# Half of pair 4's read issued before pair 3's turn, pair 6 scaled between the masks of pairs 4 and 5, pair 3's output evacuated in four parts

## The chip, the cores and the metric

The kernel runs on one core of one Trainium2 chip. The core has five engines that run side by side, each through its own list of instructions in order: TensorE (PE in the profile; PEld is its weight load), VectorE (DVE), ScalarE (ACT), GpSimd (POOL) and SyncE (SP), which here only issues transfers. The metric is the device time of one execution in microseconds, lower is better; the figure for a kernel is the median over its runs.

## The reference

A chunked state-space scan over 4 sequences of 768 tokens and 8 heads (head dimension 32, state 16) makes a matrix of 3072 tokens by 256. A gated feed-forward network follows. Cut to what matters:

```python
for c in range(nc):                                  # chunks of the sequence
    cum = np.cumsum(log_a[:, :, sl], axis=-1)
    L = np.exp(cum[:, :, :, None] - cum[:, :, None, :]) * causal
    CB = np.einsum('bhin,bhjn->bhij', Cc, Bc)
    y_intra = np.einsum('bhij,bhjd->bhid', CB * L, xc)
    y_inter = np.einsum('bhin,bhnd->bhid', Cc, state) * np.exp(cum)[:, :, :, None]
    y[:, :, sl] = y_intra + y_inter
    state = decay_full * state + np.sum(Bx, axis=2)
x = y.transpose(0, 2, 1, 3).reshape(B * S, H * D)    # 3072 x 256
gate = np.maximum(x @ w_gate, 0.0)                   # 256 x 1536
val = x @ w_val
out = gate * val @ w_out                             # 1536 x 256
```

## The kernel before

Tokens go in 12 pairs of 256 (a pair is two blocks of 128; three pairs make a sequence) for the scan, and in 6 blocks of 512 (two pairs) for the network. Pairs 0 to 3 are read with two neighbouring tokens in a row ("wide"), pairs 4 to 11 one block at a time.

A pair passes these steps. `load` (L107) issues its reads on SP: for pairs from 4 on, B, C and x of block 0, then B, C and x of block 1, six transfers (L120, L121). `scale_bc` (L324; for pair 3 `scale_wide`, L298) multiplies B and C by decay factors on POOL, four multiplies (L333) into one of four token tiles `tok`. `turn_dma` (L290) has SP issue one transposing transfer from `tok` to `turned`. `cast_x` (L340) casts x on POOL. On PE, `G` (`G_wide` for pair 3) forms the products of C and B out of `turned` into four banks of PSUM; `gevac` (L552) brings them to SBUF with the causal mask, two of them by a copy on ACT and a mask on POOL (`causal`, L547), two on DVE; pair 3 uses `gcopy` and `gmask`. `sums` (L573) adds up the states on PE out of `tok` and the cast x; `states` masks them on DVE. `inter` (L617, `inter_full` for pair 3) and `Dm` (L629, `D_wide`) add the parts of y on PE; `yevac` (`yevac_wide` for pair 3, L524) writes y as bf16 to `yT`, a tile of 128 x 2 x 3072 (its second dimension is called t here).

A block of 512 tokens passes `gv` or its half `gvh` (L655, L669) for each f of 12: gate and value products out of `yT` on PE, a relu on ACT, a product on DVE into `h`; then `fout` (L691, 12 matmuls for each of four slices of 128 tokens) and `foevac` (L710), whose writes SP issues. `gvh` takes 256 tokens, so block 1's first half reads pair 2 alone, its second half pair 3.

The order on every engine is the order in which the code is written out: `in_order` (L15) chains all instructions of an engine. So a waiting instruction holds everything behind it on its engine, and SP's list of transfers is one queue. The order around the change is in L869 to L981: after pair 3's scaling come its turn, the six reads of pair 4 and the six of pair 5 (L869 to L871), then two output writes of block 0. In block b = 1 (loop at L914, P = 4, Q = 5) pair 4 is scaled and turned, pair 6 read, pair 5 scaled and turned, pair 7 read (L942 to L949); then `G(4)` and its masks (L959, L962), later `G(5)` and its masks (L975, L976), the last slice's write, and pair 6's scaling, turn and cast (L981). Block 2 reads pairs 8 and 9 first (L917 to L919), then scales pair 7 (L946).

PSUM has a shared pool of five banks for `G`, gate, value and `fout`; `raw` holds four pairs' reads, `att` four `turned` tiles and three casts of x.

Of the kernel before, what the change touches and what calls it, by code (L numbers as in the profile page):

```python
# [8 lines left out]
FP32 = mybir.dt.float32  # L9
# [20 lines left out]
def kernel(  # L30
# [13 lines left out]
    nc = tc.nc  # L44

    NB, NH, S, D = x.shape
    N = B.shape[-1]
# [11 lines left out]
    raw = ctx.enter_context(tc.tile_pool(name="raw", bufs=4))  # L59
# [17 lines left out]
    st = {}  # L77
# [16 lines left out]
    def load_x(p, *qs):  # L94
        xr = raw.tile([128, NH, 2, D], FP32, tag="xr", name="xr")
        if p == 2:
            nc.vector.memset(xr[0:1, 0, 0, 0:1], 0.0)
        b, s0 = p // PPB, p % PPB * 256
        n = NH // len(qs)
        for i, q in enumerate(qs):  # L100
            hs = slice(i * n, (i + 1) * n)
            q.dma_start(out=xr[:, hs].rearrange("p h r d -> p h (r d)"),
                        in_=x[b, hs, s0:s0 + 256, :].rearrange(
                            "h (p r) d -> p h (r d)", r=2))
        st.setdefault(p, {})["xr"] = xr

    def load(p):  # L107
        q = nc.sync
        if p < NWIDE:
            load_bc(p, 1, q)  # L110
            load_bc(p, 0, q)
            load_x(p, q)
            return
        b, c0 = p // PPB, 2 * (p % PPB)
        xr = raw.tile([128, 2, NH, D], FP32, tag="xr", name="xr")
        bcr = raw.tile([128, 2, 2, NH, N], FP32, tag="bcr", name="bcr")
        for i in range(2):
            sl = slice((c0 + i) * 128, (c0 + i + 1) * 128)
            for src, j in ((B, 0), (C, 1)):
                q.dma_start(out=bcr[:, i, j], in_=src[b, :, sl, :].rearrange("h s n -> s h n"))  # L120
            q.dma_start(out=xr[:, i], in_=x[b, :, sl, :].rearrange("h s d -> s h d"))  # L121
        st[p] = {"xr": xr, "bcr": bcr}

    H = S // 2
    HC = NC // 2
# [24 lines left out]
    for rows, base in ((slice(0, 128), 128), (slice(0, 64), 0)):  # L150
        nc.gpsimd.affine_select(
            out=wmask[rows], in_=wmask[rows], pattern=[[-1, 2], [1, 128]],
# [6 lines left out]
    for k in range(4):  # L159
# [16 lines left out]
        out=cp0, data0=a0, data1=zero1[0:R].to_broadcast([R, 128]), initial=1.0,  # L176
# [102 lines left out]
    def scale(p, eng, ceng):  # L279
        scale_bc(p, eng)  # L280
        cast_x(p, ceng)
# [8 lines left out]
    def turn_dma(p):  # L290
        s = st[p]
        bs = tok[p % NTOK]
        s["turned"] = turned = att.tile([128, 6, 128], BF16, tag="turned", name="turned", bufs=4)
        nc.sync.dma_start_transpose(out=turned, in_=bs.rearrange("s k c -> s (k c)"))
        s["BT"] = turned[:, 0:2]
        s["CT"] = turned[:, 2:6].rearrange("s (t i) m -> s t i m", t=2)

    def scale_wide(p, j, eng):  # L298
        s = st[p]
        if p >= FIRST:  # L300
            s["bs"] = bs = tok[p % NTOK]
            src = s["bcr"].rearrange("s (t q) j r n -> s j r t q n", t=2)[:, j]
            for t in range(2):
                k = 2 * j * (1 + t)
                eng.tensor_tensor(
                    out=bs[:, k:k + 2].rearrange("s k (q t n) -> s k t q n", q=4, t=2)[:, :, t],
                    in0=src[:, :, t],
                    in1=fac3[:, j, :, 4 * t:4 * t + 4].to_broadcast([128, 2, 4, N]),
                    op=ALU.mult)
            return  # L310
        if "bs" not in s:
            s["bs"] = bs = att.tile([128, 4, 128], BF16, tag="bs", name="bs")
            s["tin"] = [[bs[:, 2 * j + r] for r in range(2)] for j in range(2)]
        src = s["bcr"].rearrange("s (t q) j r n -> s j r t q n", t=2)[:, j]
        f = wfac[:, j, :, :, p]
        for t in range(2):
            eng.tensor_tensor(  # L317
                out=s["bs"][:, 2 * j:2 * j + 2].rearrange(
                    "s k (q t n) -> s k t q n", q=4, t=2)[:, :, t],
                in0=src[:, :, t],  # L320
                in1=f[:, :, 4 * t:4 * t + 4].to_broadcast([128, 2, 4, N]),
                op=ALU.mult)
# [201 lines left out]
    def yevac_wide(p, *engs):  # L524
        s = st[p]
        for i, eng in enumerate(engs):
            dst = yT[:, :, p * 256 + i * 128:p * 256 + (i + 1) * 128]
            src = s["yw"][i][:, 0:256].rearrange("s (t m) -> s t m", t=2)
            if p >= FIRST:
                dst = dst.rearrange("s t (m r) -> s t r m", r=2)  # L530
                src = src.rearrange("s t (r m) -> s t r m", r=2)
            (eng.copy if eng is nc.scalar else eng.tensor_copy)(out=dst, in_=src)  # L532

    def G(p):
# [66 lines left out]
    def states(p):  # L601
        c = 2 * (p % PPB)
        for k in range(2 if c < NC - 2 else 1):
            S[2 * p + 1 + k] = n = att.tile([128, 2, 128], BF16, tag="Sm", name="Sm", bufs=5)
            shape = [128, 2, 4, D]
            nc.vector.tensor_tensor(  # L606
                out=n.rearrange("s t (q d) -> s t q d", q=4),
                in0=acc["A"][:, k].rearrange("s (t d) -> s t d", t=2).unsqueeze(2)
                .to_broadcast(shape),
                in1=smask.rearrange("s t (q d) -> s t q d", q=4), op=ALU.mult)  # L610
# [80 lines left out]
    def fout(b, ts, fs=range(NF)):  # L691
        if fs[0] == 0 and (ts % 2 == 0 or b == NBLK - 1):
            fst["o"] = bank("o", (128, 2, DM))
        o = fst["o"]
        if b == NBLK - 1 and ts == 3:
            fst["oh"] = [o[:, 1, 0:128], bank("o", (128, 128))]
            for i, oh in enumerate(fst["oh"]):
                for f in range(NF):
                    nc.tensor.matmul(
                        out=oh, lhsT=fst[b][:, f, ts * 128:(ts + 1) * 128],  # L700
                        rhs=wo[:, f, i * 128:(i + 1) * 128], start=(f == 0),
                        stop=(f == NF - 1), skip_group_check=True)
            return
        for f in fs:
            nc.tensor.matmul(  # L705
                out=o[:, ts % 2], lhsT=fst[b][:, f, ts * 128:(ts + 1) * 128],
                rhs=wo[:, f], start=(f == 0), stop=(f == NF - 1),
                skip_group_check=True)
# [157 lines left out]
    cast_x(2, P_)  # L866
    scale_wide(3, 1, P_)
    scale_wide(3, 0, P_)
    turn_dma(3)  # L869
    load(4)  # L870
    load(5)  # L871
    cast_x(3, P_)
    fout(0, 0)
# [40 lines left out]
    for b in range(1, NBLK):  # L914
        P, Q, W = 2 * b + 2, 2 * b + 3, 2 * b + 1
        more = P < NPAIR
        for n in (P + 2, P + 3):  # L917
            if n < NPAIR and b > 1:
                load(n)  # L919

        def at(name, *fs):

            return more and f == fs[min(b, len(fs) - 1)]

        n = 6 if b == 1 else 4
        if b > 1:
            for f in range(n):
                gvh(b, f, 0)
                if f == 1:
                    inter(W, 0)  # L930
                    inter(W, 1)
                    Dm(W)
                    if more:
                        sums(P)
                    yevac(W, nc.scalar)
                    if more:
                        states(P)
        for f in range(n):
            gvh(b, f, 1)
        for f in range(n, NF):  # L940
            gv(b, f)
            if b == 1 and at("scale P", 99, 6):  # L942
                scale(P, nc.gpsimd, nc.gpsimd)
                load(P + 2)
                inverse(2, 4)
            if at("scale Q", 9, 6, 4):  # L946
                scale(Q, nc.gpsimd, nc.gpsimd)
                if b == 1:
                    load(P + 3)  # L949
            if at("scale next P", 99, 99, 9) and P + 2 < NPAIR:  # L950
                scale(P + 2, nc.gpsimd, nc.gpsimd)
        if more:
            inter(P, 0)
            if b > 1:
                inter(P, 1)
        fout(b, 0)
        foevac(b, 0)
        if more:
            G(P)  # L959
            if b == 1:  # L960
                sums(P)
            gevac(P)  # L962
            if b == 1:
                states(P)
        fout(b, 1)
        foevac(b, 1)
        fout(b, 2)
        foevac(b, 2)
        if more:
            if b == 1:  # L970
                inter(P, 1)
            Dm(P)
            sums(Q)
            yevac(P, nc.scalar)
            G(Q)  # L975
            gevac(Q)  # L976
            states(Q)
        fout(b, 3)
        foevac(b, 3)
        if b == 1:  # L980
            scale(P + 2, nc.gpsimd, nc.gpsimd)  # L981

    in_order(tc)


# [28 lines left out]
```

## Time and profile before

| | |
|---|---|
| median of 13 runs | 127.97 us (127.12 to 129.01) |
| profiled execution | 128.37 us, of which the span of the trace is 126.7 us |
| granted TensorE clock | 1.00 |
| q1, the queue of SP | 70128 packets, 10.61 MB, 54.7% of 16 DMA engines' span |
| pair 4's tokens scaled on POOL | 35.05 to 36.54 us |
| pair 5's tokens scaled on POOL | 39.67 to 41.73 us |
| pair 6's tokens scaled on POOL | 52.35 to 53.84 us |
| turn to landing, nine turns | 2.8 to 5.7 us, median 3.8 |

Times within the trace count from the start of its span. A line of the views by order of time reads: start, length, engine, line of the kernel, operation, output<-input, and in square brackets how long the engine was idle just before, with what ended that idleness. "SPq" is SP's issuing of transfers: its length is the time that SP was held by the issue, not that of the transfer. The releaser in brackets is inferred from events, and where several things were waited for, the one that came last by the profile is named.

### The profile page before, as it was taken

How to read it: one execution, taken by the hardware profiler on the slowest of the kernel's cores; microseconds unless marked ns; L12 is line 12 of the kernel's file. 1: busy time of each engine (PE TensorE's matmuls, PEld its weight loads, DVE VectorE, ACT ScalarE, POOL GpSimd, SP SyncE). 2: the span in 40 equal slices, each digit the busy share in tenths (PEclk: the TensorE clock that was granted, in tenths of full speed). 3: DMA queues.
4: the chain of work that ended last, by engine and by line, in shares of the span. 5: the costliest groups of instructions: out<-in, count | busy, mean ns of one | idle time of the engine just before them, and what ended most of it. 6: DMA issues, size and time to landing. Idle time of an engine off the chain costs nothing.

```text
span 126.7 us, 3664 instructions
## 1 busy us (share of the span) xinstructions
PE 118.6 (94%) x1404; PEld 82.4 (65%) x1404; DVE 88.2 (70%) x199; ACT 76.5 (60%) x168; POOL 47.9 (38%) x108
## 2 busy tenths in 40 slices
PE   6989999999999896889998999999999999999990
PEld 6766784576784474775467784477874577854790
DVE  4798989772999851868854788745988854687510
ACT  0558598755977533757644687644787545876410
POOL 6599979470363330780153531502900032000000
PEclk9999999999999999999999999999999999999999
DMA  3999999947789976999999199994290002200022
GB/s 61 222 205 142 168 191 195 185 99 105 89 107 199 176 98 104 107 257 68 115 105 160 31 205 121 108 113 87 87 141 5 0 0 88 83 0 0 0 88 83
DMA packets 77489, 13.93 MB, mean 110 GB/s; under 512 B 70064, under 2 KB 77472, under 8 KB 77472
## 3 DMA queue, kind: packets, MB, share of 16 engines
q1 hardware_dynamic: 70128, 10.61, 54.7%
q0 software_dynamic: 4288, 2.36, 13.9%
q10 hardware_dynamic: 3056, 0.72, 2.6%
q8 instruction: 11, 0.18, 0.6%
q14 instruction: 6, 0.05, 0.1%
HBM read 11.13 MB, written 3.15 MB: 113 GB/s over the span
## 4 chain that ended last, share of the span: by engine, by line
PE 73%; DMA 8%; POOL 6%; DVE 5%; ACT 2%; issue 1%; SPq 1%; POOLq 0%; DVEq 0%
PE o L705 19%; PE gv L678 16%; PE val L663 13%; PE gate L660 13%; DMA turned<-tok 8%; DVE h L684 3%; PE g L540 2%; PE w L184 2%; POOL wg L194 2%; DVE gs L428 1%; PE y L635 1%; POOL bs L317 1%; ACT gs L559 1%; POOL tok L333 1%; PE y L624 1%
## 5 line engine op out<-in xcount | busy, mean ns | idle before, releaser
L667 DVE TENSOR_TENSOR h<-r,val 128x512 bf16<-128x512 bf16 x44 | 30.0, 684 | 7.4 <-ACT r L666 7.2
L705 PE MATMUL o<-wo,h 128*128 128x256 bf16 x276 | 33.1, 273 | 0.0
L666 ACT ACTIVATE r<-gate 128x512 bf16<-128x512 f32 x44 | 26.3, 597 | 9.7 <-PE gate L660 9.3
L705 PEld LDWEIGHTS <-h 128*128 128x128 bf16 x276 | 25.9, 98 | 5.3 <-issue 1.7
L663 PE MATMUL val<-yT,wv 128*128 128x512 bf16 x88 | 26.2, 379 | 0.0
L660 PE MATMUL gate<-yT,wg 128*128 128x512 bf16 x88 | 26.2, 379 | 0.0
L684 DVE TENSOR_TENSOR h<-r,gv 128x256 bf16<-128x256 bf16 x56 | 22.8, 419 | 2.9 <-ACT r L681 2.3
L681 ACT ACTIVATE r<-gv 128x256 bf16<-128x256 f32 x56 | 21.2, 386 | 4.0 <-PE gv L678 2.1
L678 PE MATMUL gv<-yT,wg 128*128 128x256 bf16 x112 | 21.6, 273 | 0.4 <-DVE yT L532 0.4
L678 PE MATMUL gv<-yT,wv 128*128 128x256 bf16 x112 | 21.4, 273 | 0.0
L548 POOL TENSOR_SCALAR_AFFINE_SELECT gs<-gs 128x512 bf16<-128x512 bf16 (+1 forms) x16 | 8.0, 524 | 34.0 <-ACT gs L559 34.0
L565 DVE TENSOR_TENSOR gs<-g,maskUT 128x512 bf16<-128x512 f32 x16 | 10.3, 686 | 13.7 <-issue 8.7
L333 POOL TENSOR_TENSOR tok<-bcr,scaleBC 128x128 bf16<-128x128 f32 x32 | 12.0, 405 | 15.6 <-DMA bcr<-in_B_dram 12.2
L663 PEld LDWEIGHTS <-wv 128*128 128x128 bf16 x88 | 8.6, 98 | 10.4
L660 PEld LDWEIGHTS <-wg 128*128 128x128 bf16 x88 | 8.6, 98 | 8.9
L678 PEld LDWEIGHTS <-wv 128*128 128x128 bf16 x112 | 10.9, 98 | 1.5 <-DMA wv<-in_moe_w_val_dram 0.3
L678 PEld LDWEIGHTS <-wg 128*128 128x128 bf16 x112 | 10.3, 98 | 2.2 <-DVE yT L532 0.6
L559 ACT CAST gs<-g 128x512 bf16<-128x512 f32 x8 | 4.7, 588 | 8.7 <-PE g L540 8.7
L648 ACT CAST yT<-y 128x512 bf16<-128x512 f32 x8 | 4.7, 586 | 5.1 <-PE y L635 2.5
L428 DVE TENSOR_TENSOR gs<-g,wmask 128x512 bf16<-128x512 f32 x9 | 5.9, 681 | 2.6 <-PE g L413 2.6
L606 DVE TENSOR_TENSOR Sm<-A_ps,smask 128x256 bf16<-128x256 f32 x15 | 5.7, 414 | 1.0 <-PE A_ps L593 1.0
L184 PE MATMUL w<-warm 128*128 128x128 bf16 x49 | 5.4, 279 | 1.1 <-DVE tmask L158 1.1
(121 smaller groups left out, 114.8 us busy)
## 6 DMA issues: line engine op xcount, KB each, us to landing
xr<-in_x_dram SPq DMA_DIRECT2D x17, 128.0 KB, 3.3
out_dram<-ob SPq DMA_DIRECT2D x3, 512.0 KB, 3.8
bcr<-in_C_dram SPq DMA_DIRECT2D x17, 64.0 KB, 3.0
bcr<-in_B_dram SPq DMA_DIRECT2D x17, 64.0 KB, 3.0
out_dram<-ob SPq DMA_DIRECT2D x4, 256.0 KB, 2.5
xr<-in_x_dram SPq DMA_DIRECT2D x3, 256.0 KB, 3.9
wo<-in_moe_w_out_dram POOLq DMA_DIRECT2D x2, 384.0 KB, 8.9
wg<-in_moe_w_gate_dram POOLq DMA_DIRECT2D x4, 128.0 KB, 4.7
```

The costliest lines, as they stand in the source:

```text
L184: nc.tensor.matmul(out=w, lhsT=warm, rhs=rhs, start=True, stop=True)
L333: eng.tensor_tensor(out=dst[:, t, j * (1 + t)], in0=src[:, j, :, t], in1=f[:, j, :, 4 * t:4 * t + 4].to_broadcast([128, 2, 4, N]), op=ALU. ...
L548: nc.gpsimd.affine_select(out=dst, in_=dst, pattern=[[0, n], [1, 128]], compare_op=ALU.is_ge, fill=0.0, base=0, channel_multiplier=-1)
L565: nc.vector.tensor_tensor(out=d[:, q], in0=g[q], in1=m, op=ALU.mult)
L660: nc.tensor.matmul(out=g, lhsT=wg[:, k, fs], rhs=yT[:, k, tk], start=(k == 0), stop=(k == 1))
L663: nc.tensor.matmul(out=v, lhsT=wv[:, k, fs], rhs=yT[:, k, tk], start=(k == 0), stop=(k == 1))
L666: nc.scalar.activation(r, g, AF.Relu)
L667: nc.vector.tensor_tensor(out=fst[b][:, f], in0=r, in1=v, op=ALU.mult)
L678: nc.tensor.matmul(out=gv_[:, j], lhsT=w[:, k, fs], rhs=yT[:, k, tk], start=(k == 0), stop=(k == 1), skip_group_check=True)
L681: nc.scalar.activation(r, gv_[:, 0], AF.Relu)
L684: nc.vector.tensor_tensor(out=fst[b][:, f, u * 256:(u + 1) * 256], in0=r, in1=gv_[:, 1], op=ALU.mult)
L705: nc.tensor.matmul(out=o[:, ts % 2], lhsT=fst[b][:, f, ts * 128:(ts + 1) * 128], rhs=wo[:, f], start=(f == 0), stop=(f == NF - 1), skip_gr ...
```

## The change

Three edits. `load` takes a list of blocks, and pair 4's first block is read ahead of pair 3's turn, its second behind it. Pair 6's scaling, turn and cast, so far at the end of block 1, stand in it behind pair 4's masks and states and ahead of pair 5's masks; on SP pair 6's turn so comes ahead of block 1's output write. `yevac_wide` of pair 3 copies each of its two halves in two parts, one for each t, on the same engines: ACT and DVE have one instruction more each. No transfer and no matmul is added or left out.

```diff
-    def load(p):
+    def load(p, parts=(0, 1)):
...
-        xr = raw.tile([128, 2, NH, D], FP32, tag="xr", name="xr")
-        bcr = raw.tile([128, 2, 2, NH, N], FP32, tag="bcr", name="bcr")
-        for i in range(2):
+        if p not in st:
+            st[p] = {"xr": raw.tile([128, 2, NH, D], FP32, tag="xr", name="xr"),
+                     "bcr": raw.tile([128, 2, 2, NH, N], FP32, tag="bcr", name="bcr")}
+        xr, bcr = st[p]["xr"], st[p]["bcr"]
+        for i in parts:
...
-        st[p] = {"xr": xr, "bcr": bcr}
...
             if p >= FIRST:
-                dst = dst.rearrange("s t (m r) -> s t r m", r=2)
-                src = src.rearrange("s t (r m) -> s t r m", r=2)
+                for t in range(2):
+                    (eng.copy if eng is nc.scalar else eng.tensor_copy)(
+                        out=dst[:, t].rearrange("s (m r) -> s m r", r=2),
+                        in_=src[:, t].rearrange("s (r m) -> s m r", r=2))
+                continue
...
     scale_wide(3, 0, P_)
+    load(4, (0,))
     turn_dma(3)
-    load(4)
+    load(4, (1,))
     load(5)
...
             gevac(P)
             if b == 1:
                 states(P)
+                scale(P + 2, nc.gpsimd, nc.gpsimd)
         fout(b, 1)
...
         foevac(b, 3)
-        if b == 1:
-            scale(P + 2, nc.gpsimd, nc.gpsimd)
-
```

## The prediction

> **What bounds the kernel now.** I read the busy table first, then PE's busy time by stage, then PE's order of time where it pauses, then the queue of SP, then POOL.
>
> ```profile
> PE 118.6 (94%) x1404; PEld 82.4 (65%) x1404; DVE 88.2 (70%) x199; ACT 76.5 (60%) x168; POOL 47.9 (38%) x108
> ```
>
> PE is the busiest engine, so time can come only from its pauses. Stage by stage (window, its length, then busy us of PE, PEld, DVE, ACT, POOL, then granted clock and DMA share):
>
> ```profile
> 34.00:54.50 20.50, 17.65 (x232) 12.21 (x227) 14.39 (x32) 11.78 (x25) 8.30 (x20) 1.00 0.86 127
> 54.50:70.00 15.50, 14.96 (x154) 9.68 (x153) 10.41 (x19) 9.12 (x18) 4.99 (x12) 1.00 1.07 144
> 70.00:88.00 18.00, 18.00 (x196) 12.19 (x188) 12.98 (x25) 11.49 (x24) 6.08 (x14) 1.00 0.78 113
> ```
>
> From 70 us PE does not pause until the last microseconds. Between 34 and 70 it is idle for 20.50 - 17.65 + 15.50 - 14.96 = 3.39 us, at the granted clock of 1.00. PE's order of time gives five pauses (in brackets: idle just before, and what ended it):
>
> ```profile
> 34.93 0.28 PE L678 MATMUL gv<-yT,wg 128*128 128x256 bf16 x1 [0.42 <-DVE yT L532]
> ...
> 43.60 0.29 PE L624 MATMUL y<-turned,Sm 128*128 128x128 bf16 x2 [0.37 <-DMA turned<-tok]
> ...
> 50.25 0.40 PE L540 MATMUL g<-turned 32*128 32x256 bf16 x8 [1.12 <-DMA turned<-tok]
> ...
> 54.44 0.27 PE L593 MATMUL A_ps<-xb,tok 128*32 128x64 bf16 x12 [0.94 <-POOL xb L348]
> ...
> 69.82 0.40 PE L540 MATMUL g<-turned 32*128 32x256 bf16 x8 [0.54 <-DMA turned<-tok]
> ```
>
> 0.42 + 0.37 + 1.12 + 0.94 + 0.54 = 3.39 us. Three wait for a turned tile: pairs 4, 5 and 7. The turns are issued by SP, so its queue (start, duration of the issue):
>
> ```profile
> 23.99 0.81 SPq L102 DMA_DIRECT2D xr<-in_x_dram  x1
> 27.36 1.31 SPq L294 DMA_TRANSPOSE turned<-tok  x1
> 28.72 0.57 SPq L120 DMA_DIRECT2D bcr<-in_B_dram  x1
> 29.34 0.57 SPq L120 DMA_DIRECT2D bcr<-in_C_dram  x1
> 30.01 0.54 SPq L121 DMA_DIRECT2D xr<-in_x_dram  x1
> 30.59 1.05 SPq L120 DMA_DIRECT2D bcr<-in_B_dram  x1
> ...
> 40.03 1.28 SPq L294 DMA_TRANSPOSE turned<-tok  x1
> ...
> 46.40 2.27 SPq L294 DMA_TRANSPOSE turned<-tok  x1
> ...
> 65.49 0.95 SPq L121 DMA_DIRECT2D xr<-in_x_dram  x1
> 66.54 2.55 SPq L294 DMA_TRANSPOSE turned<-tok  x2
> ```
>
> SP stands idle from 23.99 + 0.81 = 24.80 to 27.36, 2.56 us, because pair 3's turn waits for pair 3's tok. From 27.36 to the turn of pair 7 at 66.54 one issue follows another with no gap over 0.1 us. The tokens of pairs 4, 5 and 7 are scaled well before their turns start (POOL ends them at 36.54, 41.73 and 55.83, the turns start at 40.03, 46.40 and 66.54). So the turns are late only because SP comes to them late; where the chain of waits puts ACT or POOL before them, that is a releaser inferred from what ended near. The fourth pause is POOL's order:
>
> ```profile
> 51.38 1.00 POOL L548 TENSOR_SCALAR_AFFINE_SELECT gs<-gs 128x512 bf16<-128x512 bf16 x2 [4.17 <-ACT gs L559]
> 52.35 1.49 POOL L333 TENSOR_TENSOR tok<-bcr,scaleBC 128x128 bf16<-128x128 f32 x4
> 53.77 0.62 POOL L348 CAST xb<-xr 128x512 bf16<-128x512 f32 x1
> ```
>
> Pair 6's scaling and cast stand behind pair 5's masks, for which POOL idles 4.17 us.
>
> **Part 1, half of pair 4's read moved ahead of pair 3's turn.** No instruction is added. Three reads (B, C, x of one block) leave 28.72 to 30.59, 1.87 us of the unbroken queue, and go into the idle 2.56 us. In the new place they cost between 1.83 us (28.72 to 30.55 now) and 3.67 us (the longest three in a row, 30.59 to 34.26). Nearest are the four reads just ahead, 21.34 to 24.80: 3.46 / 4 = 0.865 each, 2.60 for three. So pair 3's turn is issued 0.04 us later and all behind it 1.87 - 0.04 = 1.83 us earlier. Low end: 3.67 us makes it 1.87 - 1.11 = 0.76. High end: the twelve reads of pairs 4 and 5 take 10.03 us (28.72 to 38.75), 0.84 each, and if nine go at that mean, 2.51 are saved. I take 1.83, say 1.8. The turn also lands later behind new traffic. It now lands 2.8 us after its issue, with the queue empty ahead; the turns directly behind a read need 3.2 (pair 7), 3.8 (pair 5) and 4.3 to 4.5 (pair 9, at 82.49), pair 6's, behind a 512 KB write, 5.7. I take the middle one, 3.8: 27.40 + 3.8 = 31.2, where PE reaches G of pair 3 at 30.79 now. Charge 0.4 us; none at 2.8, 33.1 - 30.8 = 2.3 us at 5.7. What stands behind G there is the whole of PE, and the masks on DVE, ACT and POOL.
>
> A rule speaks against this part: the Trainium skill, "DMA: Bandwidth & Descriptors", section "Queues, rings and completion order", says that each DMA engine consumes descriptors in ring order, so a turn cannot overtake reads issued before it. An estimate from it: three reads of 8 x 128 packets at 15.8 ns (54.7% of 16 engines over 126.7 us, by 70128 packets) are 3.0 us on 16 engines; starting at 27, where the DMA share drops to 0.07, they end at 30.0, the turn about 1.5 later, and PE would lose 0.7 us rather than 0.4; by the sum below either is paid out of a later pause.
>
> **Part 2, the evacuation of pair 3 in four parts.** At 34.93 PE runs the group of f = 5 of the first half block, which reads pair 2's tokens alone, yet its second weight load waits for DVE and its matmul for ACT. In the changed program these waits stand one group later, at the first that reads pair 3's own tokens: one copy of both t spans an address range that covers pair 2's t = 1, a copy of one t does not. Cost: ACT 128x256 447 ns becomes two of 128x128 (the nearest row, L733: 266 ns), +0.08; DVE 444 becomes 2 x 290, +0.14. So the last part ends at 34.43 + 0.58 = 35.01 and the second matmul of pair 3's group, now at about 35.38, can start at 35.06: 0.3 us of the 0.42 come free. Bounds: 0.42, and 0 if the banks that DVE frees become late by its 0.14.
>
> **Part 3, pair 6 scaled between the two masks.** Four multiplies (1.49) and a cast (0.62) move ahead of masks 5, and on SP pair 6's turn moves ahead of block 1's output write. The new wait is POOL's for pair 6's second half. It is issued now at 43.29 to 46.30 and landed by about 48.5; 1.8 earlier that is 46.7, when masks 4 are over (47.2 less some 0.5). Scaling then ends about 48.8, while ACT's copy for masks 5 ends about 49.7 (now 51.32). So nothing is delayed behind it, and the 0.94 us go. If that cover fails, masks 5, then y of pair 5 on PE, wait.
>
> **Sum along PE.** G of pair 3: -0.4. Evacuation: +0.3, so 0.1 behind. Pair 4's turn lands at 43.56 - 1.8 = 41.8, its 0.37 goes: 0.27 ahead. Pair 5's lands at 50.21 - 1.8 = 48.4, PE is there at 49.13 - 0.27 = 48.9, its 1.12 goes: 1.39. Pair 6's cast: 2.33. But pair 7's turn lands at 69.77 - 1.8 = 68.0 and PE is there at 69.28 - 2.33 = 66.95: a pause of 1.0 us in place of 0.54. From there PE is 1.8 us early to the end, as it has no later pause. The profiled execution took 128.37 us, 126.7 of span and 1.67 around it: 128.37 - 1.8 = 126.57. The median of the runs is 127.97, 0.40 lower: 126.17, so 126.2. Parts 2 and 3 bring nothing at the end by this sum; they lie in the new pause.
>
> **Rivals.** (a) *SP stops being the limit.* If more of the queue's time than 1.87 is saved, PE gets what its pauses give: at 2.51 the time is 127.97 - 2.5 = 125.5, at most 127.97 - (-0.1 + 0.37 + 1.12 + 0.94 + 0.54 = 2.87) = 125.1. For it: reads issued just after a turn are the short ones. Against: DMA share 1.07 from 54.5 to 70. (b) *The read is not really earlier.* The DMA share is 0.82 to 0.99 from 24 to 27, so the moved reads may hold SP for 3.67 us, and pair 3's turn for 2.27 in place of 1.31: 1.87 - 1.11 - 0.96 = -0.2, so 127.4 to 128.2, about 128.0. Against: DMA share is 0.07 at 27 to 28 and 0.36 at 28 to 29. (c) *Slower: the rings stay one half read deeper.* Each turn then lands as late as pair 6's, 5.7 us after issue. It decides at pair 7's turn, from a lag of 3.2 + 1.83 = 5.06 us: 66.54 - 1.83 + 5.7 = 70.4, +0.6, 128.6; with the saving at 0.76, +1.7, 129.7. For it: the row of 5.7. Against: that row stands behind a 512 KB write, and no turn behind a read shows more than 4.5.
>
> **How the numbers follow.** Forecast 0.58, (a) 0.12, (b) 0.17, (c) 0.13. What this kernel's measurement can tell from no change is about 0.5%, 0.64 us. The forecast's own range is the saving's, 0.76 to 2.51: 125.5 to 127.2. To leave out no more than 2 in 10 I go to 125.0 to 127.9: (c) lies outside, and little of (a) and (b). Faster: forecast and (a), 0.70; same: (b), 0.17; slower: (c), 0.13.
>
> **What would show it.** Right: three reads in SP's queue between 24.8 and 27.5; pair 7's turn issued near 64.7; PE's pauses before L624 of pair 4, L540 of pair 5 and the sums of pair 6 gone, and that before G of pair 7 grown to about 1.0 us. Wrong: pair 3's turn issued after 28, or landing after 31.5 with a pause before G of pair 3; masks of pair 5 starting after 52; or pair 7's turn still near 66.5. If the pause before G of pair 7 is gone as well, (a) holds.

## The result and the profile after

The changed kernel takes 126.53 us in the median of 11 runs, before 127.98 in 48; run against run the ratio is 0.9867 with a 95% interval of 0.9836 to 0.9897, so 1.3% less. Disturbed executions, with a lower granted clock or late transfers, do not count in the ratios nor in the medians below, which is why some kernels have few; without them the changed kernel's median is 126.4 and before's 128.2. The profiled execution of the changed kernel took 126.94 us with a span of 125.1.

PE by stage in the changed kernel (columns as before: window, length, busy us of PE, PEld, DVE, ACT, POOL, clock, DMA share):

```profile
34.00:54.50 20.50, 19.60 (x257) 14.05 (x256) 15.81 (x38) 13.10 (x30) 10.21 (x24) 1.00 1.00 140
54.50:70.00 15.50, 14.57 (x141) 9.25 (x139) 10.12 (x18) 8.95 (x18) 3.81 (x10) 1.00 0.78 115
```

Between 34 and 54.5 us PE idles 0.90 us, where it had idled 2.85, and the DMA share there went from 0.86 to 1.00. In the next window it idles 0.93, where it had idled 0.54. PE's order of time shows which pauses are left:

```profile
31.14 0.42 PE L414 MATMUL g<-turned 32*64 32x256 bf16 x16 [0.44 <-DMA turned<-tok]
...
43.03 0.28 PE L628 MATMUL y<-turned,Sm 128*128 128x128 bf16 x2
...
49.45 0.40 PE L544 MATMUL g<-turned 32*128 32x256 bf16 x8 [0.90 <-DMA turned<-tok]
...
52.52 0.26 PE L597 MATMUL A_ps<-xb,tok 128*32 128x64 bf16 x12
...
68.28 0.40 PE L544 MATMUL g<-turned 32*128 32x256 bf16 x8 [0.93 <-DMA turned<-tok]
```

The pause at pair 3's evacuation, that before pair 4's first matmul (0.37) and that before pair 6's sums (0.94) are gone. A new one of 0.44 stands before G of pair 3. Pair 5's is 0.90 instead of 1.12, pair 7's 0.93 instead of 0.54. SP's queue in the changed kernel:

```profile
24.77 0.58 SPq L122 DMA_DIRECT2D bcr<-in_B_dram  x1
25.39 0.89 SPq L122 DMA_DIRECT2D bcr<-in_C_dram  x1
26.38 1.71 SPq L123 DMA_DIRECT2D xr<-in_x_dram  x1
28.19 1.32 SPq L295 DMA_TRANSPOSE turned<-tok  x1
...
38.55 1.27 SPq L295 DMA_TRANSPOSE turned<-tok  x1
...
44.45 1.23 SPq L295 DMA_TRANSPOSE turned<-tok  x1
...
64.99 2.56 SPq L295 DMA_TRANSPOSE turned<-tok  x2
```

The three reads hold SP from 24.77 to 28.09. Pair 3's turn is issued 0.83 later than before, pair 4's 1.48 earlier, pair 5's 1.95, pair 7's 1.55. This execution also started 0.16 earlier (first fout matmul at 23.72, before at 23.88). A figure free of the start is the stage from the first fout matmul to G of pair 7: 45.94 us before, 44.56 after, 1.38 less. From G of pair 7 to the end it is 56.88 and 56.82: of the 1.6 us between the two spans, 1.38 lie in this stage and 0.16 in the start.

### The profile page after: what moved, and what is told of

The parts are those of the page before. It is cut to its first block, busy times and chain, and to the rows that moved or that the text cites. A ratio compares the mean times of both kernels' runs of the same rounds, so it can differ in the third digit from the quotient of the medians.

```text
span 125.1 us, 3665 instructions
## 1 busy us (share of the span) xinstructions
PE 118.2 (94%) x1404; PEld 82.4 (66%) x1404; DVE 88.0 (70%) x200; ACT 76.5 (61%) x169; POOL 48.2 (39%) x108
## 4 chain that ended last, share of the span: by engine, by line
PE 70%; DMA 12%; SPq 6%; POOL 4%; DVE 1%; ACT 1%; issue 1%; DVEq 0%; POOLq 0%
PE gv L682 20%; PE o L709 15%; PE gate L664 12%; PE val L667 11%; DMA turned<-tok 9%; DMA xr<-in_x_dram 3%; SPq L122 2%; PE w L185 2%; PE g L544 2%; POOL wg L195 2%; PE y L639 2%; SPq L89 2%; POOL bs L318 1%; PE y L628 1%; PE o L703 1%
## 5 line engine op out<-in xcount | busy, mean ns | idle before, releaser
L185 PEld LDWEIGHTS <-warm 128*128 128x128 bf16 x58 | 5.0, 126 | 1.7 <-DVE tmask L159 1.1
```

What stands on the lines that cost most here:

```text
L185: nc.tensor.matmul(out=w, lhsT=warm, rhs=rhs, start=True, stop=True)
```

## The experiments

Three theories. Theory 1: PE's own path and SP's queue run side by side and the later one sets G of pair 7. Theory 2: each pause removed is worth its length at the end. Theory 3: the DMA engines are the limit, and a turn lands no earlier for standing earlier in the queue. "Stage" is that of the last paragraph, from the profiled execution of each kernel; times are medians, or the times themselves where there are two or three.

| kernel | time, us | ratio to before, 95% | stage, us |
|---|---|---|---|
| before | 128.2 | | 45.94 |
| changed | 126.4 | 0.9867 (0.9836 to 0.9897) | 44.56 |
| half read ahead alone | 127.6 | 0.9976 (0.9938 to 1.0014) | 44.51 |
| the same again | 127.55 | 0.9943 (0.9908 to 0.9978) | 44.59 |
| the other two edits alone | 127.74, 128.14, 128.44 | no interval | 45.29 |
| changed, pair 7's turn moved | 126.24 | 0.9859 (0.9814 to 0.9904) | 43.05 |
| changed, pair 5's turn moved | 125.75, 126.39 | 0.9846 (0.977 to 0.9922) | none |
| changed, both turns moved | 124.8 | 0.9727 (0.9679 to 0.9774) | none |
| both turns moved, no read ahead | 126.0 | 0.9833 (0.9791 to 0.9874) | 43.63 |
| both turns moved, two copies | 125.8 | 0.9816 (0.9782 to 0.9850) | 42.86 |
| changed, two reads ahead | 126.25, 126.66 | 0.9853 (0.9783 to 0.9923) | 43.97 |
| changed, long rows | 125.98, 126.65 | 0.9853 (0.9801 to 0.9906) | 43.63 |

**The half read ahead alone.** The other two edits are undone; the lines that undo the evacuation in four parts are left out here.

```diff
...
             if b == 1:
                 states(P)
-                scale(P + 2, nc.gpsimd, nc.gpsimd)
...
+        if b == 1:
+            scale(P + 2, nc.gpsimd, nc.gpsimd)
```

> Only the half read ahead is kept; pair 6 is scaled after pair 5's masks and pair 3 is evacuated in two copies, as before. Theory 1 (the end is set by pair 7's turn, which comes when SP's queue comes to it): the pauses before the first group of pair 2's tokens (0.4 us) and before the sums of pair 6 (0.9) come back, but PE then only reaches G of pair 7 about 0.9 us later than in the changed kernel, where it pauses 0.93 for the turn: time 126.5 to 126.8, pause before G of pair 7 near 0. Theory 2 (every pause that goes is worth its length at the end): 126.5 + 0.3 + 0.9 = 127.7.

Measured: 127.6 us. PE's order of time in its profiled execution, which took 126.94:

```profile
31.26 0.42 PE L414 MATMUL g<-turned 32*64 32x256 bf16 x16 [0.42 <-DMA turned<-tok]
...
35.40 0.28 PE L679 MATMUL gv<-yT,wg 128*128 128x256 bf16 x1 [0.42 <-DVE yT L533]
...
53.39 0.27 PE L594 MATMUL A_ps<-xb,tok 128*32 128x64 bf16 x12 [0.94 <-POOL xb L349]
...
68.36 0.40 PE L541 MATMUL g<-turned 32*128 32x256 bf16 x8
```

This is theory 1's picture: the pauses of 0.42 and 0.94 are back, that before G of pair 7 is gone, and the stage, 44.51, is that of the changed kernel. But this was its fastest execution; the median is theory 2's, 1.2 us above the changed kernel's. A second profile of the same kernel:

> preread_alone once more, whose profiled execution was its fastest (126.94 us) while most took 127.3 to 128.5: a profile of one more execution. If the later of the two paths sets the time: whatever it takes above 126.9 stands as a longer pause before G of pair 3, 5 or 7 or as a later start, with the 0.42 and 0.94 us pauses in both.

The profiled execution took 126.94 again, the stage 44.59, with pauses of 0.34, 0.42, 0.52 (before G of pair 5) and 0.94 and none before G of pair 7; and this too was its fastest execution; the others took 127.18 to 127.98. What those lose stands in no trace.

**The other two edits alone.**

```diff
-    load(4, (0,))
     turn_dma(3)
-    load(4, (1,))
+    load(4)
```

> The other two edits are kept, pair 4 is read behind pair 3's turn as before. Theory 1: SP's queue is that of before, pair 7's turn is issued near 66.5 us and the time is that of before, 128.0 (127.6 to 128.2), with a pause before G of pair 7 of 0.54 + 0.3 + 0.94 = 1.8 us. Theory 2: 128.0 - 0.3 - 0.94 = 126.8.

One time, 127.74 us, which is too little to go by; the same kernel once more:

> The same kernel as without_preread, whose first executions were nearly all disturbed (one undisturbed: 127.74 us). Theory 1 (SP's queue and PE's own path run side by side, the later one sets G of pair 7): SP's queue is that of before, so 127.6 to 128.2. Theory 2 (pauses add up): 126.8.

128.14 and 128.44: no faster than before, against theory 2's 126.8. PE's order of time in the second run, and one line of its SP queue:

```profile
43.66 0.28 PE L628 MATMUL y<-turned,Sm 128*128 128x128 bf16 x2 [0.47 <-DMA turned<-tok]
...
50.17 0.40 PE L544 MATMUL g<-turned 32*128 32x256 bf16 x8 [0.98 <-DMA turned<-tok]
...
69.51 0.40 PE L544 MATMUL g<-turned 32*128 32x256 bf16 x8 [1.44 <-DMA turned<-tok]
```

```profile
65.90 2.61 SPq L295 DMA_TRANSPOSE turned<-tok  x2
```

The pauses at pair 3's evacuation and pair 6's sums are gone, 1.36 us, and the three turns take 0.86 of it back (0.47 + 0.98 + 1.44 against 0.37 + 1.12 + 0.54). Pair 7's turn is issued at 65.90, before at 66.54, and G of pair 7 waits for it. The stage is 0.65 shorter, but this execution started 0.34 later and has one more pause, 0.30 before G of pair 9. Of the four combinations, the half read gives some 0.6 us (the interval of one of its two ratios takes in no change at all), the other two edits nothing that three executions can tell, all three 1.8: the edits need each other. Neither theory holds throughout: theory 2 has the half read's time right, theory 1 that of the other two edits.

**Pair 7's turn between the reads of pairs 8 and 9.**

```diff
-            if n < NPAIR and b > 1:
+            if n < NPAIR and b > 1 and (b > 2 or n == P + 2):
                 load(n)
...
-                if b == 1:
+                if b <= 2:
                     load(P + 3)
```

> The changed kernel with pair 7's turn issued between the reads of pairs 8 and 9 instead of behind both. Theory 1: the turn is issued near 60 us, the pause of 0.93 us before G of pair 7 goes, 125.6. Rival 3 (the DMA engines are the limit, a turn lands no earlier for standing earlier in the queue, or pair 8's turn becomes late in its place): 126.5 or more.

SP's queue, and G of pair 3 and pair 7 on PE:

```profile
61.15 1.22 SPq L295 DMA_TRANSPOSE turned<-tok  x1
```

```profile
32.38 0.42 PE L414 MATMUL g<-turned 32*64 32x256 bf16 x16 [0.84 <-DMA turned<-tok]
...
67.60 0.40 PE L544 MATMUL g<-turned 32*128 32x256 bf16 x8
```

The turn goes out 3.8 us earlier, lands 3.1 us after its issue (3.2 in the changed kernel), and the pause before G of pair 7 is gone: theory 3 falls for this turn. The stage is 43.05, 1.51 less than in the changed kernel, but the edit accounts for only 0.93 of it, the pause it removes. Pair 5's pause of 0.90 is gone as well, because pair 5's turn landed 3.6 us after issue instead of 5.0, which the edit does not touch; G of pair 3 waited 0.40 longer. The time is 126.24, only 0.2 less; the execution that left the trace, of 126.17, started later (first fout matmul at 24.55). So the pause agrees with theory 1 and the time falls short of its 125.6.

**Pair 5's turn ahead of pair 6's read.**

```diff
                 scale(P, nc.gpsimd, nc.gpsimd)
-                load(P + 2)
                 inverse(2, 4)
...
                 if b == 1:
+                    load(P + 2)
                     load(P + 3)
```

> The changed kernel with pair 5's turn issued ahead of pair 6's read. Theory 1: the pause of 0.90 us before G of pair 5 goes, but pair 7's turn keeps its place in SP's queue, so the pause before G of pair 7 grows from 0.93 to about 1.8 us and the time stays 126.5. Theory 2: 126.5 - 0.9 = 125.6.

Its two times, 125.75 and 126.39, lie between theory 1's 126.5 and theory 2's 125.6, and no trace shows either: inconclusive.

**Both turns moved.**

> The changed kernel with pair 5's turn ahead of pair 6's read and pair 7's turn between the reads of pairs 8 and 9. Theory 1: no turn of pairs 5 or 7 is waited for, PE's own path is left: from the first fout matmul to G of pair 7 about 43.1 us, time 125.3 to 126.1 with the start's spread of 0.8. Theory 3 (the DMA engines are the limit; the reads of pairs 6 and 9 that now come later are waited for instead): 126.5 or more.

Four executions took 124.65 to 125.1 us: 0.9727 of before, 1.6 us below the changed kernel and somewhat below theory 1's range. It beats both kernels. Pair 7's move alone gave 0.2 us, the two together 1.6. No trace shows any of the four, so how the two moves share the gain, and where the path is now the longest, is not shown.

**Both turns moved, pair 4 read wholly behind pair 3's turn.**

> Both turns moved as in both_turns_first, but pair 4 read wholly behind pair 3's turn, as before. Theory 1 (a turn is late by its place in SP's queue, so moving the turns makes the half read ahead unneeded): only the 0.4 us before pair 4's first matmul are left of the pauses for turns, and the pause before G of pair 3 goes: 125.0 to 125.9, within 0.9 of both_turns_first (124.8). Rival: the reads themselves, 1.9 us later, are waited for (pair 6's cast stands ahead of pair 5's masks on POOL): 126.5 or more.

```profile
44.14 0.29 PE L628 MATMUL y<-turned,Sm 128*128 128x128 bf16 x2 [1.37 <-DMA turned<-tok]
```

```profile
40.06 2.60 SPq L295 DMA_TRANSPOSE turned<-tok  x2
```

The first of these lines is the only pause of PE in the stage. 126.0 us is just outside theory 1's range and below the rival's, and 1.2, not at most 0.9, above the kernel with the half read: the read ahead is not unneeded, and in this theory 1 was wrong. It is now pair 4's turn, issued at 40.06, for which PE comes 1.37 us early.

**Both turns moved, pair 3 evacuated in two copies.**

> both_turns_first with pair 3 evacuated in two copies, as before. With the turns out of the way PE's own path is the limit, so the pause before the second weight load of pair 2's last group (0.42 us) comes back and shows at the end at its full worth: 124.8 + 0.3 = 125.1. If the four copies are worth nothing (DVE's and ACT's extra 0.1 us give it back): 124.8.

125.8 us, 1.0 above both_turns_first; 0.3 was expected. Its profile shows the pause once more:

```profile
31.52 0.42 PE L414 MATMUL g<-turned 32*64 32x256 bf16 x16 [0.31 <-DMA turned<-tok]
...
35.67 0.28 PE L679 MATMUL gv<-yT,wg 128*128 128x256 bf16 x1 [0.42 <-DVE yT L533]
```

0.42 us are shown by this; the other 0.6 are not in it.

**Two reads ahead instead of three.**

```diff
-    load(4, (0,))
+    load(4, (0,), "bc")
     turn_dma(3)
+    load(4, (0,), "x")
```

> The changed kernel with only B and C of pair 4's first block ahead of pair 3's turn, x behind it. The three reads held SP for 3.3 us in its idle stretch and put the turn off by 1.0. Theory 1: two reads hold it about 1.5 us, the turn goes out when its tokens are ready (about 3.4 us after the last read of pair 3 was issued, near 27.2), no pause before G of pair 3, and pair 7's turn is at most 0.4 earlier or later than 65.0: 126.1 to 126.6. Rival: the third read is worth its 0.6 us in the queue: 127.1.

SP's queue and G of pair 3:

```profile
24.91 0.58 SPq L123 DMA_DIRECT2D bcr<-in_B_dram  x1
25.53 0.86 SPq L123 DMA_DIRECT2D bcr<-in_C_dram  x1
27.23 2.63 SPq L297 DMA_TRANSPOSE turned<-tok  x1
29.97 0.52 SPq L125 DMA_DIRECT2D xr<-in_x_dram  x1
```

```profile
31.45 0.42 PE L416 MATMUL g<-turned 32*64 32x256 bf16 x16 [0.75 <-DMA turned<-tok]
```

The turn goes out at 27.23, as theory 1 said, but now it holds SP for 2.63 us instead of 1.32, and SP is free at 29.86 (29.51 in the changed kernel). The pause before G of pair 3 is longer, not gone. The time, 126.25 and 126.66, is as expected. So a hold is not the price of the instruction that shows it: with the third read behind it, the turn is held 1.31 us more. It would fit that SP waits for transfers ahead of it that are unfinished; no trace shows what it waits for.

**Long rows for pairs 8 and 9.**

```diff
+            if p in (8, 9):
+                for src, j in ((B, 0), (C, 1)):
+                    q.dma_start(out=bcr[:, i, j].rearrange("s h n -> s (h n)"),
+                                in_=src[b].rearrange("h s n -> (h s n)")[0:128 * NH * N].rearrange(
+                                    "(s c) -> s c", s=128))
...
+                continue
```

> The changed kernel, but the twelve reads of pairs 8 and 9 take the same bytes in rows of 512 B (B, C) and 1 KB (x) instead of 64 B and 128 B, 128 rows each instead of 1024; they read other tokens. Where the number of rows that the DMA engines have to move sets how long a read holds SP: about 0.57 us each, 7.4 us for twelve instead of 11.6, pair 7's turn out near 61 instead of 65, no pause before G of pair 7. Where each issue costs SP its time whatever the rows: twelve reads still take 11 to 12 us, turn near 65, pause as in the changed kernel.

SP's queue at the end of these reads:

```profile
59.26 0.43 SPq L123 DMA_DIRECT2D bcr<-in_C_dram  x1
59.73 0.43 SPq L126 DMA_DIRECT2D xr<-in_x_dram  x1
60.27 2.55 SPq L304 DMA_TRANSPOSE turned<-tok  x2
```

These reads are of other tokens, so the output is not the network's. Twelve reads take from 53.69 to 60.16, 6.5 us instead of 11.5 (53.34 to 64.88), and the last nine hold SP for 0.43 us each. The pause before G of pair 7 is gone and the stage is 43.63, 0.93 less than in the changed kernel. It is the rows, whose number and length change together here, not the bytes or the count of issues, that fill SP's queue. The Trainium skill, "Perfetto Trace Analysis", section "DMA Optimizations", says that small DMAs, below 2 KB, have a significant overhead per transfer. These transfers are of 64 and 128 KB in both kernels; if a row is taken for what the page calls a transfer, the runs agree in direction, with rows of 64 and 128 B against 512 B and 1 KB, and no run here shows the limit of 2 KB.

**The changed kernel again.**

> The changed kernel once more, for the spread between executions: 126.5 us; from the first fout matmul to G of pair 7 between 43.9 and 44.6 us (44.56 in its first profile, 45.94 before), from there to the end 56.8 to 56.9.

Four executions took 125.83 to 127.01 us, median 126.3. None of the four has a trace, so the stage that was expected could not be read.

## Why the prediction was right, and where it was not

*The time.* 126.53 against 126.2, within the range: a gain of 1.45 us between the medians of all runs, 1.7 by the ratio; 1.8 was predicted. That it came out so is partly luck, as the step that failed shows below. Rivals (b) and (c) are out: the queue is ahead by 1.55 us at pair 7's turn, which lands 3.2 us after issue as before. (The lag of 5.06 us in rival (c) is 3.23 + 1.83; with the 3.2 written there it would be 5.03.) Rival (a) is out as well for the traced execution, since a pause of 0.93 us is left there.

*The half read.* The mechanism was right, two of its sizes were not. The three reads held SP 3.32 us, not 2.60, inside the bound of 3.67: pair 3's turn went out at 28.19 instead of 27.40, past the 28 that the prediction had named as a sign against it. Against that, it landed 2.9 us after issue, not 3.8. The errors cancel by luck: the pause before G of pair 3 is 0.44, predicted 0.4. The estimate from ring order, the Trainium skill's "DMA: Bandwidth & Descriptors", section "Queues, rings and completion order", was 0.7. That section gives the order in which an engine takes up descriptors, and says that a later one may finish its write first; in this trace the turn did not overtake the reads, the last of which landed at 30.3, the turn at 31.1. That the rest of the wait had moved into SP's issue would fit the longer hold, but is not shown.

*The saving in the queue.* 1.55 us at pair 7's turn, of which 0.16 is an earlier start, against 1.83. At pair 5's turn it was 1.95, but this turn landed 5.0 us after issue instead of 3.8: with the DMA share in that stage up from 0.86 to 1.00, its pause stayed at 0.90 where 0 was predicted.

*The evacuation.* Right in kind, and dearer by less. The copies in the changed kernel, ACT's and DVE's:

```profile
34.73 0.43 ACT L532 CAST yT<-y 128x128 bf16<-128x128 f32 x2
```

```profile
34.79 0.49 DVE L532 CAST yT<-y 128x128 bf16<-128x128 f32 x2
```

Two parts, which overlap, take 0.43 on ACT (one copy took 0.447) and 0.49 on DVE (0.444), so the cost was 0 and 0.05 instead of 0.08 and 0.14. The wait did move one group later, as predicted: pair 2's last group on PE starts at 34.59 and 34.81 while the copies still run, to 35.28, and the next weight load, for the first group that reads pair 3's tokens, waits for DVE:

```profile
35.13 0.29 PEld L682 LDWEIGHTS <-wg 128*128 128x128 bf16 x2 [0.21 <-DVE yT L532]
```

One reading was off: at 34.93 in the kernel before, the trace names DVE, not ACT, as what the matmul waited for too.

*The masks.* Right: pair 6's scaling ended before pair 5's masks were ready.

```profile
46.60 1.49 POOL L334 TENSOR_TENSOR tok<-bcr,scaleBC 128x128 bf16<-128x128 f32 x4
48.59 0.61 POOL L349 CAST xb<-xr 128x512 bf16<-128x512 f32 x1 [0.51 <-PE A_ps L597]
50.59 1.00 POOL L552 TENSOR_SCALAR_AFFINE_SELECT gs<-gs 128x512 bf16<-128x512 bf16 x2 [1.39 <-ACT gs L563]
```

POOL idled 1.39 us before the masks. The 0.51 us before the cast were given to PE; they were the read of x, issued at 43.59 and landed 4.9 us later, at 48.5.

*The step that failed* is "Parts 2 and 3 bring nothing at the end by this sum; they lie in the new pause". In the profiled executions it seems to hold: the half read alone has a stage of 44.51 and 44.59, the changed kernel 44.56. But each of the three took 126.94 us, which is the fastest of the half read's executions and half a microsecond above the changed kernel's median, so they are not typical of either. In the times it failed: without the two edits the median is 127.6, with them 126.4. By the prediction's sum the half read alone would have brought the whole 1.8 us; it brought some 0.6, less than the low end of 0.76, and that the total was right is luck to that extent. The sum treated one execution's landings as fixed. They are not: pair 5's turn took 5.0 us to land in the changed kernel, 3.8 before and 3.6 with pair 7's turn moved, and the start moves by up to 0.8. When the two paths lie within a microsecond of each other, taking something off either may then help in some executions. This is argued, not shown: how the 1.2 us divide, and whether they all lie in this stage, no trace shows, and it stays open. What the times show is that the two edits without the half read bring nothing that could be told, and with it 1.2 us.

## What to carry to other kernels

Look in the queue that issues transfers, not only at the engine that is named as releaser: a transfer whose data have long been ready is late by its place, and moving it ahead of reads that nobody needs yet can be worth as much as moving a read (here 1.6 us for two turns, on top of the changed kernel, and 1.2 for the half read, on top of the moved turns). Where two paths run side by side within a microsecond, measure edits together and apart: one pause removed may only lengthen the next. In this kernel one copy over both t held up matmuls that read other tokens, and one copy for each t did not; that the span of addresses is what counts is argued from this.

## What was not expected of the hardware

A read of 1024 rows held SP between 0.4 and 2.2 us in the two traces of before and after, a read of 128 rows and the same bytes 0.43 in nine of twelve cases and 0.60 to 0.89 in the first three. A turn held it between 1.22 and 2.81 in the traces of all kernels. The hold is not fixed by the instruction: with one read fewer in front, pair 3's turn took 2.63 instead of 1.32, and SP was free no earlier.
